# Weight conversion through PSUM banks, and decay and mask products in 64-row form, in an attention and two-expert-layer kernel

## The chip, the cores and the metric

The kernel runs on one core of a Trainium2 chip. A core has five engines with a queue each: TensorE (PE in the rows; its weight loads are PEld), VectorE (DVE), ScalarE (ACT), GpSimd (POOL) and SyncE (SP), which here issues the DMA transfers. SBUF is the working memory, PSUM holds TensorE's sums in eight banks. The metric is the device time of one execution in microseconds (us).

## The reference

```python
scores = scale * np.matmul(q, k.transpose(0, 1, 3, 2))      # 4 batches, 8 heads, 576 x 576, head size 64
cum = np.cumsum(np.log(np.clip(f, 0.0001, 1.0)), axis=-1)
scores = np.where(causal, -1e9, scores + cum[..., :, None] - cum[..., None, :])
attn = softmax(scores)                                      # over the last axis
x = (attn @ v)  ->  [2304, 512]                             # tokens by 8 heads x 64
h = np.maximum(x @ w_in, 0.0); x = h * h @ w_out            # w_in [512, 2048], w_out [2048, 512]
# router: logits + softplus(x @ w_noise) * noise, the two best of 8 experts per token
out[mask] += top2_w * (np.maximum(x[mask] @ w1[e], 0.0) @ w2[e])
```

## The kernel before

Every matrix is carried as a high and a low part in 16 bits (hi and lo), and a product is three matmuls: hi x hi, hi x lo, lo x hi (`HL3`). The program has three parts that overlap.

**Attention.** The first 256 queries of each batch are done by head units (`hd_tick`: `hd_s`, `hd_split`, `hd_pv`; 12 of them), the other 320 by units of two heads and 128 queries, or 64 for the last (`att_tick`: `att_s`, `att_exp`, `att_split`, `att_pv`; 48 of them). A unit's scores of its two heads (z = 0, 1) lie in two PSUM banks: three key products per head with 64 rows (contraction over the head size), then the decay product, whose 24 rows hold the three 16-bit pieces of the cumulated logarithms of 8 heads (`crow`) and a selector (`esel`), then the causal mask, an identity times a triangle (`identb`, `masku`, 128 rows). In units of 64 queries a bank holds both heads, side by side in partitions, for half of the keys. VectorE takes the maximum, ScalarE the exponential, GpSimd the low part, a DMA transposes, and TensorE multiplies by v.

**First layer.** `w_in` and `w_out` come as 64-bit floats in blocks, two halves for each of 16 values of i (`load_w`, SyncE). `conv_w` makes a 32-bit float of each from its two words in three VectorE steps (lines 434 to 436), with a scratch tile `w32` in SBUF, the result in place in the load's buffer `w64`; ScalarE makes the high part (line 443) and VectorE the low part (line 444). There are three load buffers. Ten of the 32 conversions are issued with the first head units (`weights_ahead`), the rest ahead of the steps that use them. `mm1` and `mm2` then go over chunks of 384 tokens and i: passes over chunk 0 and 1 with i from 0 to 7 (pass 0 and 1), again with i from 8 to 15 (pass 2 and 3), then one pass for each of the chunks 2 to 5.

**Router and experts.** From the end of the first layer on, after about 650 us; the change does not touch them.

The scores' banks are the pool tag "S" with three buffers, which rotate; at the start two more (tag "X") join, and `start_bank` and `main_bank` hand them out. A scheduler at build time sets the order of the instructions on each engine from the program's order, its dependences and its pools; each engine then runs its queue in that order.

Of the kernel before, what the change touches and what calls it, by code (L numbers as in the profile page):

```python
# [52 lines left out]
def attn_moe_moe_kernel(ctx: ExitStack, tc, qka, qk, v, f, w_io, wgn, noise, w1, w2, out):  # L53
# [59 lines left out]
    nc.gpsimd.affine_select(identb, identb, [[-1, 128]], ALU.not_equal, 1.0, base=0, channel_multiplier=1)  # L113
    nc.gpsimd.memset(masku, 0.0)
    nc.gpsimd.affine_select(masku, masku, [[-1, 128]], ALU.is_ge, -BIG, base=0, channel_multiplier=1)

# [22 lines left out]
    for z in range(2):  # L139
        es = esel[64 * z:64 * z + 24]  # L140
        nc.gpsimd.memset(es, -8.0)
        nc.gpsimd.affine_select(es, es, [[-3, 8], [0, 128]], ALU.is_ge, 0.0, base=0, channel_multiplier=1)
        nc.gpsimd.affine_select(es, es, [[3, 8], [0, 128]], ALU.is_ge, 0.0, base=2, channel_multiplier=-1)
    ident2k = consts.tile([128, 128], F16, name="ident2k")
# [32 lines left out]
    def att_s(u, pools):  # L177
        b, i, p = u
        n = p
        st[u] = [pool.tile([128, 512], F32, name="ps", tag=tag, bufs=bufs) for pool, tag, bufs in pools]  # L180
        q0 = S + 128 * i - HEAD
        if i < 4:
            N = 128 * (i + 1)
            for x, (qi, ki) in enumerate(HL3):
                for z in range(2):
                    r = slice(64 * z, 64 * z + 64)
                    nc.tensor.matmul(st[u][z][:, :N], QK[n][r, qi, q0:q0 + 128], QK[n][r, ki, :N], start=(x == 0), stop=False)  # L187
            for z in range(2):
                r = slice(64 * z, 64 * z + 24)
                nc.tensor.matmul(st[u][z][:, :N], esel[r, 2 * p + z], crow[r, b, :N], start=False, stop=False)  # L190
            for z in range(2):
                nc.tensor.matmul(st[u][z][:, N - 128:N], identb, masku, start=False, stop=True)  # L192
        else:
            for hf in range(2):
                ps = st[u][hf]
                ks = slice(288 * hf, 288 * hf + 288)
                for x, (qi, ki) in enumerate(HL3):
                    for z in range(2):
                        r = slice(64 * z, 64 * z + 64)
                        nc.tensor.matmul(ps[r, :288], QK[n][r, qi, q0:q0 + 64], QK[n][r, ki, ks], start=(x == 0), stop=False, skip_group_check=True)  # L200
                nc.tensor.matmul(ps[:, :288], esel.rearrange("r h t -> r (h t)")[0:24, 256 * p + 64:256 * p + 192], crow[0:24, b, ks], start=False, stop=(hf == 0), skip_group_check=True)
            for z in range(2):
                r = slice(64 * z, 64 * z + 64)
                nc.tensor.matmul(st[u][1][r, 224:288], identb[r, 64 * z:64 * z + 64], masku[r, 64 * z:64 * z + 64],
                                 start=False, stop=True, skip_group_check=True)

# [130 lines left out]
    def hd_s(u, bank):  # L337
# [13 lines left out]
        for p in range(np_):  # L351
            for z in range(2):
                r = slice(64 * z, 64 * z + 24)
                nc.tensor.matmul(ps[z][:, W * p:W * p + W], esel[r, 2 * (np_ * a + p) + z], crow[r, b, 0:W],
                                 start=False, stop=False, skip_group_check=True)
        v4 = [t.rearrange("p (c w) -> p c w", w=W) for t in ps]
        for z in range(2):
            nc.tensor.matmul(v4[z][:, :, 128 * i:128 * i + 128], identb, masku[:, None, :].to_broadcast([128, np_, 128]),
                             start=False, stop=True, skip_group_check=True)
        if a == 0:  # L360
# [451 lines left out]
    def weights_ahead(j):  # L812
        if j >= 0 and j % 2 == 0 and j // 2 < AHEAD:
            load_w(j // 2)
        if j >= 1 and (j - 1) // 2 < AHEAD:
            conv_w(("in", "out")[(j - 1) % 2], (j - 1) // 2)

# [36 lines left out]
    for s_i, (n, c, i) in enumerate(steps):  # L854
# [29 lines left out]
        for w_i in new:  # L884
            with ExitStack() as behind:
                if w_i >= NA and k:
                    behind.enter_context(tc.issue_after(seen[units[k - 1]]))
                conv_w("in", w_i)
                conv_w("out", w_i)
        if c in (2, 3) and i % 4 == 3:  # L890
# [138 lines left out]
```

## Time and profile before

| what | value |
|---|---|
| median of 3 runs | 1088.98 us (1086.57 to 1092.2) |
| the profiled execution | 1083.63 us, span 1081.9 us |
| TensorE busy | 991.0 us, 92% of the span |
| VectorE busy | 579.6 us, 54% |
| ScalarE, GpSimd busy | 443.3 us and 369.3 us |
| moved by DMA | 153.5 MB, mean 142 GB/s |

Busy time is what the engine's instructions cover of the span, not work at full speed: a matmul's end is modelled, and it includes the way through the array. The mean over the span hides that the first 200 us and the rest have different limits.

### The profile page before, as it was taken

The page shows a single profiled execution, that of the slowest core. Times are in us where ns is not written, and L with a number is a line of the kernel's source. Part 1 is how long each engine was busy: PE and PEld are TensorE (multiplying, and loading weights), DVE is VectorE, ACT ScalarE, POOL GpSimd, SP SyncE. Part 2 cuts the span into 40 slices and gives each one's busy share as a digit, 9 for nine tenths or more (in the row PEclk, how much of TensorE's full clock was granted, in tenths as well). Part 3 has the DMA queues.
Part 4 walks back from the last instruction along what each step waited for, and adds up shares of the span by engine and source line. Part 5 has one row for each costly group of instructions (what it writes and reads, how often), then busy time and mean ns, then how long its engine had stood idle before and what let it go on. Part 6 is the DMA issues. An engine that isn't in the chain of part 4 may idle for free.

```text
span 1081.9 us, 18041 instructions
## 1 busy us (share of the span) xinstructions
PE 991.0 (92%) x7050; PEld 537.5 (50%) x7050; DVE 579.6 (54%) x1159; ACT 443.3 (41%) x989; POOL 369.3 (34%) x331
## 2 busy tenths in 40 slices
PE   3748898899999999999998989998999999999996
PEld 1425444455454554555454434446646474646563
DVE  8998899624766666665537614214734343433121
ACT  3756676644555554564336312003513131412020
POOL 7454632311546535623410230533232404030202
PEclk9999899999999999999999989999999999999999
DMA  7599999433766784672529462437995938370303
GB/s 275 162 201 194 264 224 232 104 76 77 146 141 145 186 176 86 135 144 36 93 40 311 156 155 59 69 69 153 322 214 160 210 93 214 97 148 10 49 1 50
DMA packets 240393, 153.50 MB, mean 142 GB/s; under 512 B 194066, under 2 KB 204626, under 8 KB 240306
## 3 DMA queue, kind: packets, MB, share of 16 engines
q1 hardware_dynamic: 230194, 131.32, 50.3%
q0 software_dynamic: 10112, 21.02, 10.4%
q8 instruction: 56, 0.92, 0.4%
q14 instruction: 31, 0.25, 0.1%
HBM read 81.63 MB, written 24.30 MB: 98 GB/s over the span
## 4 chain that ended last, share of the span: by engine, by line
PE 62%; DVE 16%; DMA 9%; issue 6%; ACT 3%; POOL 2%; SPq 1%; ACTq 0%; POOLq 0%; DVEq 0%
PE e L753 18%; PE e L740 16%; PE m L456 10%; PE acc L500 9%; DMA wr<-in_w_dram 3%; DMA w<-in_w_io_dram 2%; DVE w L435 2%; PE ps L187 2%; DVE w L436 1%; DVE w L434 1%; PE po L282 1%; DVE r L466 1%; DVE wout L444 1%; DVE sm L217 1%; PE ps L200 1%
## 5 line engine op out<-in xcount | busy, mean ns | idle before, releaser
L740 PE MATMUL e<-xgT,w1s 128*128 128x320 f16 (+2 forms) x1536 | 217.8, 302 | 7.1 <-DMA xgT<-xg 5.0
L456 PE MATMUL m<-xT,win 128*128 128x384 f16 x1152 | 209.7, 332 | 13.7 <-ACT r L460 13.1
L500 PE MATMUL acc<-wout,g 128*128 128x512 f16 x864 | 205.6, 380 | 11.2 <-DVE g L464 6.3
L753 PE MATMUL e<-w2s,hT 128*128 128x512 f16 x960 | 212.1, 380 | 3.9 <-ACT hT L744 3.9
L740 PEld LDWEIGHTS <-w1s 128*128 128x128 f16 x1536 | 143.5, 99 | 80.7 <-issue 13.7
L456 PEld LDWEIGHTS <-win 128*128 128x128 f16 x1152 | 110.0, 99 | 88.8 <-issue 23.3
L753 PEld LDWEIGHTS <-hT 128*128 128x128 f16 x960 | 93.7, 98 | 114.0 <-ACT hT L744 4.2
L500 PEld LDWEIGHTS <-g 128*128 128x128 f16 x864 | 81.8, 98 | 102.2 <-DVE g L464 10.8
L744 ACT ACTIVATE hT<-e 128x320 f16<-128x320 f32 (+2 forms) x128 | 53.9, 435 | 186.3 <-PE e L740 186.2
L757 POOL DMA_INDIRECT out_dram<-y,tix x40 | 63.9, 1598 | 142.9 <-DVE y L756 134.7
L745 DVE SCALAR_TENSOR_TENSOR hT<-e,hT 128x320 f16<-128x320 f32 (+2 forms) x128 | 60.4, 487 | 96.0 <-ACT hT L744 95.8
L756 DVE TENSOR_SCALAR y<-e,gs 128x512 f32<-128x512 f32 x40 | 30.0, 750 | 146.0 <-PE e L753 131.6
L466 DVE TENSOR_TENSOR r<-r 128x384 f32<-128x384 f32 x64 | 56.8, 888 | 90.7 <-ACT g L461 90.7
L241 POOL TENSOR_TENSOR phl<-pr,phl 128x384 f16<-128x384 f32 (+1 forms) x64 | 68.7, 1090 | 81.6 <-issue 59.8
L460 ACT ACTIVATE r<-m 128x384 f32<-128x384 f32 x96 | 46.6, 486 | 90.9 <-PE m L456 85.4
L706 POOL DMA_INDIRECT xg<-x2d,tix x40 | 44.7, 1117 | 113.4 <-DMA xgT<-xg 103.5
L641 POOL DMA_INDIRECT table<-ent,si x36 | 36.1, 1002 | 127.8 <-DVE si L638 99.0
L676 ACT ACTIVATE w2s<-wr 128x1024 f16<-128x1024 f32 x32 | 32.5, 1050 | 106.3 <-PE e L753 88.5
L217 DVE TENSOR_REDUCE sm<-ps 128x1 f32<-128x384 f32 (+2 forms) x96 | 51.7, 561 | 34.0 <-PE ps L192 20.8
L220 ACT ACTIVATE pr<-ps,sm 128x384 f32<-128x384 f32 (+1 forms) x64 | 40.0, 627 | 57.7 <-DVE sm L219 56.1
L349 PE MATMUL psab<-hs 64*128 64x128 f16 (+1 forms) x192 | 27.7, 342 | 26.2 <-ACT pr L371 14.7
L461 ACT ACTIVATE g<-r 128x384 f16<-128x384 f32 x96 | 50.2, 522 | 1.8
(253 smaller groups left out, 1160.0 us busy)
## 6 DMA issues: line engine op xcount, KB each, us to landing
wr<-in_w_dram SPq DMA_DIRECT2D x64, 512.0 KB
w<-in_w_io_dram SPq DMA_DIRECT2D x32, 512.0 KB
qkr<-in_qk_dram SPq DMA_DIRECT2D x16, 448.0 KB
vr<-in_v_dram SPq DMA_DIRECT2D x16, 320.0 KB
x2d<-x SPq DMA_DIRECT2D x18, 256.0 KB
qkh<-in_qka_dram SPq DMA_DIRECT2D x8, 512.0 KB
out_dram<-zero SPq DMA_DIRECT2D x5, 768.0 KB
vh<-in_v_dram SPq DMA_DIRECT2D x8, 256.0 KB
```

The source lines that it names most:

```text
L217: seen[u] = nc.vector.tensor_reduce(sm[:, z:z + 1], ps[z][:, :N], AX.X, ALU.max).ins
L241: nc.gpsimd.tensor_tensor(lo, pv, hi, op=ALU.subtract)
L456: nc.tensor.matmul(ps, win[i][:, cc, wi, :], xT[:, xi, cc, r0:r0 + CH], start=(x == 0), stop=(x == 11))
L460: nc.scalar.activation(r, ps, AF.Relu)
L461: nc.scalar.activation(g[:, 0, :], r, AF.Square, scale=2.0 ** -10)
L466: nc.vector.tensor_tensor(r, r, r, op=ALU.mult)
L500: nc.tensor.matmul(acc[t], g[:, gi, 128 * t:128 * t + 128], wout[i][:, wi, :], start=(i in ends[c][0] and x == 0), stop=(i in ends[c][1] a ...
L740: nc.tensor.matmul(ps[:, :hw], w1s[:, cc, wi, 128 * i:128 * i + 128], xgT[:, 4 * xi + cc, hw * q:hw * q + hw], start=(x == 0), stop=(x == 11))
L744: nc.scalar.activation(hi, ps[:, :hw], AF.Relu)
L745: nc.vector.scalar_tensor_tensor(hT[:, i, 1, hw * q:hw * q + hw], ps[:, :hw], 0.0, hi, op0=ALU.max, op1=ALU.subtract)
L753: nc.tensor.matmul(ps, hT[:, i, hi, 128 * j:128 * j + 128], w2s[:, i, wi, :], start=(i == 0 and x == 0), stop=(i == NFE - 1 and x == 2))
L757: s_ = nc.gpsimd.indirect_dma_start(out=out, out_offset=bass.IndirectOffsetOnAxis(ap=tix[:, j, 0:1], axis=0), in_=y, in_offset=None, compu ...
```

## The change

It does three things. The conversion's scratch and its result go to a PSUM bank, taken from `start_bank` or `main_bank` as the scores take theirs; so `w32` is gone, the load's buffer is only read, and ScalarE and VectorE read the result from PSUM. The decay product gets 64 rows instead of 24: `crow` is cleared first, so that the rows 24 to 63 of each half add nothing, and the selector is one column per head, repeated over the 128 (or 64) columns of the weight load by its access pattern. The mask product is split in two halves of 64 rows, the identity and the triangle lying in each half of the partitions. The low parts of the probabilities are made on GpSimd, as before.

```diff
-    identb = consts.tile([128, 128], BF16, name="identb")
-    masku = consts.tile([128, 128], BF16, name="masku")
-    esel = apool.tile([128, H, 128], F16, name="esel")
+    identb = consts.tile([128, 2, 128], BF16, name="identb")
+    masku = consts.tile([128, 2, 128], BF16, name="masku")
+    esel = apool.tile([128, H], F16, name="esel")
     crow = apool.tile([128, B, S], F16, name="crow")
+    nc.gpsimd.memset(crow, 0.0)
...
+    def decay(r, h, m):
+        return esel[r, h:h + 1].to_broadcast([64, m])
...
             for z in range(2):
-                r = slice(64 * z, 64 * z + 24)
-                nc.tensor.matmul(st[u][z][:, :N], esel[r, 2 * p + z], crow[r, b, :N], start=False, stop=False)
-            for z in range(2):
-                nc.tensor.matmul(st[u][z][:, N - 128:N], identb, masku, start=False, stop=True)
+                r = slice(64 * z, 64 * z + 64)
+                nc.tensor.matmul(st[u][z][:, :N], decay(r, 2 * p + z, 128), crow[r, b, :N], start=False, stop=False)
+            for hf in range(2):
+                for z in range(2):
+                    r = slice(64 * z, 64 * z + 64)
+                    nc.tensor.matmul(st[u][z][:, N - 128:N], identb[r, hf], masku[r, hf], start=False, stop=(hf == 1))
...
-                nc.tensor.matmul(ps[:, :288], esel.rearrange("r h t -> r (h t)")[0:24, 256 * p + 64:256 * p + 192], crow[0:24, b, ks], start=False, stop=(hf == 0), skip_group_check=True)
+                for z in range(2):
+                    r = slice(64 * z, 64 * z + 64)
+                    nc.tensor.matmul(ps[r, :288], decay(r, 2 * p + z, 64), crow[r, b, ks], start=False, stop=(hf == 0), skip_group_check=True)
...
-    def conv_w(kind, i):
+    def conv_w(kind, i, bank):
         t = wst.pop((kind, i))
-        u = astream.tile([128, 512], I32, name="w32", bufs=1)
+        w_ = bank()
+        u = w_.bitcast(I32)
         nc.vector.tensor_scalar(u, t[:, :, 1], 3, 0x3FFFFFF8, op0=ALU.logical_shift_left, op1=ALU.bitwise_and)
         nc.vector.scalar_tensor_tensor(u, t[:, :, 1], -0x40000000, u, op0=ALU.bitwise_and, op1=ALU.bitwise_or)
-        nc.vector.scalar_tensor_tensor(t[:, :, 0], t[:, :, 0], 29, u, op0=ALU.logical_shift_right, op1=ALU.bitwise_or)
-        w_ = t.bitcast(F32)[:, :, 0]
+        nc.vector.scalar_tensor_tensor(u, t[:, :, 0], 29, u, op0=ALU.logical_shift_right, op1=ALU.bitwise_or)
```

The head units (`hd_s`) get the same two changes as the units of 128 queries. Lines after the constants stand some 7 to 12 lines further down in the changed kernel (434 to 436 and 444 are 447 to 449 and 456 there).

On VectorE, where pass 1 begins (the conversions of i = 8 and 9; w64 is the load's buffer, w32 the scratch, sm and ps belong to an attention unit), the order before is:

```order
L435 SCALAR_TENSOR_TENSOR w32_1602<-w64_1538,w32_1602 128x512
L217 TENSOR_REDUCE sm_1713<-ps_1702 128x1
L219 TENSOR_SCALAR sm_1713<-sm_1713 128x1
L436 SCALAR_TENSOR_TENSOR w64_1538<-w64_1538,w32_1602 128x512
L219 TENSOR_SCALAR sm_1713<-sm_1713 128x1
L434 TENSOR_SCALAR w32_1608<-w64_1540 128x512
L435 SCALAR_TENSOR_TENSOR w32_1608<-w64_1540,w32_1608 128x512
L444 SCALAR_TENSOR_TENSOR win8_155<-w64_1538,win8_155 128x4x128
L436 SCALAR_TENSOR_TENSOR w64_1540<-w64_1540,w32_1608 128x512
```

and in the changed kernel (psab are banks of the scores, here taken by conversions, xs and vs belong to the attention):

```order
L447 TENSOR_SCALAR psab_1635<-w64_1569 128x512
L447 TENSOR_SCALAR psab_1641<-w64_1571 128x512
L229 TENSOR_SCALAR sm_1627<-sm_1627 128x1
L448 SCALAR_TENSOR_TENSOR psab_1635<-w64_1569,psab_1635 128x512
L448 SCALAR_TENSOR_TENSOR psab_1641<-w64_1571,psab_1641 128x512
L449 SCALAR_TENSOR_TENSOR psab_1635<-w64_1569,psab_1635 128x512
L447 TENSOR_SCALAR psab_1682<-w64_1647 128x512
L449 SCALAR_TENSOR_TENSOR psab_1641<-w64_1571,psab_1641 128x512
L309 TENSOR_TENSOR xs_1514<-po_1435,sums_1197 128x512
L178 SCALAR_TENSOR_TENSOR vs_1729<-vr_1600,vs_1729 128x10x64
L448 SCALAR_TENSOR_TENSOR psab_1682<-w64_1647,psab_1682 128x512
```

A conversion's first step now stands before the last step of up to two others, each with a bank of its own, and no attention unit's maximum stands between them.

On TensorE, in a unit of 64 queries late in the attention (set is q and k of a head pair, ps the two banks of the unit), the order before is:

```order
L200 MATMUL ps_4123<-set2_1693 64x288
L201 LDWEIGHTS esel_98
L201 MATMUL ps_4123<-crow_99,esel_98 128x288
L200 LDWEIGHTS set2_1693
L200 MATMUL ps_4124<-set2_1693 64x288
```

and in the changed kernel:

```order
L209 MATMUL ps_4198<-set2_1726 64x288
L212 LDWEIGHTS esel_98
L212 MATMUL ps_4198<-crow_99,esel_98 64x288
L212 LDWEIGHTS esel_98
L212 MATMUL ps_4198<-crow_99,esel_98 64x288
L209 LDWEIGHTS set2_1726
L209 MATMUL ps_4199<-set2_1726 64x288
```

The decay product of 128 partitions between key products of 64 has become two of 64 partitions, in the same shape as the products around it.

On TensorE, in a unit of 128 queries in the second pass over chunk 0 before, and in pass 1 in the changed kernel (ps_2110 and ps_2111 are the banks of one unit's two heads, ps_1857 is the bank of one head), the order before is:

```order
L187 MATMUL ps_2110<-set0_1561 128x512
L187 LDWEIGHTS set0_1561
L187 MATMUL ps_2111<-set0_1561 128x512
L190 LDWEIGHTS esel_98
L190 MATMUL ps_2110<-crow_99,esel_98 128x512
L190 LDWEIGHTS esel_98
L190 MATMUL ps_2111<-crow_99,esel_98 128x512
L192 LDWEIGHTS identb_96
L192 MATMUL ps_2110<-masku_97,identb_96 128x128
L192 LDWEIGHTS identb_96
L192 MATMUL ps_2111<-masku_97,identb_96 128x128
```

and in the changed kernel:

```order
L194 MATMUL ps_1857<-set2_1726 128x384
L194 LDWEIGHTS set2_1726
L194 MATMUL ps_1857<-set2_1726 128x384
L194 LDWEIGHTS set2_1726
L194 MATMUL ps_1857<-set2_1726 128x384
L197 LDWEIGHTS esel_98
L197 MATMUL ps_1857<-crow_99,esel_98 128x384
L201 LDWEIGHTS identb_96
L201 MATMUL ps_1857<-masku_97,identb_96 128x128
L201 LDWEIGHTS identb_96
L201 MATMUL ps_1857<-masku_97,identb_96 128x128
```

Before, the two heads' products alternate; in the changed kernel one head's key, decay and mask products stand alone here, with two mask products for one.

## Rows read from the trace of the kernel before

**Rows 1.** stretches: length, busy us (instructions) of PE, PEld, DVE, ACT, POOL, clock, DMA
```profile
25.00:61.00 36.00, 21.67 (x144) 12.48 (x145) 33.29 (x46) 20.14 (x62) 18.97 (x8) 1.00 0.58 163
61.00:122.00 61.00, 44.93 (x352) 25.35 (x352) 54.06 (x75) 41.01 (x114) 29.65 (x19) 0.95 1.05 224
122.00:200.00 78.00, 70.83 (x529) 35.77 (x528) 71.76 (x128) 51.34 (x118) 26.18 (x22) 0.98 0.85 212
200.00:513.00 313.00, 304.70 (x2584) 159.59 (x2583) 178.72 (x466) 166.91 (x398) 129.57 (x130) 1.00 0.57 123
```

**Rows 2.** SyncE's waits from 14 to 216 us: total, times, longest
```profile
SPq L428 <- DVE wout L444: 17.1, 9, 5.0
SPq L428 <- DVE win L444: 14.3, 6, 9.7
```

**Rows 3.** VectorE's timeline, 37 to 52 us: start, duration, instruction
```profile
42.09 2.49 DVE L435 SCALAR_TENSOR_TENSOR w<-w,w 128x512 int32<-128x512 int32 x1
44.50 0.68 DVE L366 TENSOR_REDUCE smh<-psab 128x2 f32<-128x512 f32 x1
...
50.01 0.69 DVE L435 SCALAR_TENSOR_TENSOR w<-w,w 128x512 int32<-128x512 int32 x1
```

**Rows 4.** GpSimd's timeline, 36 to 52 us
```profile
39.12 4.91 POOL L327 TENSOR_TENSOR hs<-qkh,hs 128x1024 f16<-128x1024 f32 x2
43.99 5.10 POOL L381 TENSOR_TENSOR phlh<-pr,phlh 128x1024 f16<-128x1024 f32 x2
```

**Rows 5.** single lines: count, ns least/median/most, first and last start
```profile
L434 DVE TENSOR_SCALAR w<-w x32: 408/426/2336, 14.3 to 193.8; 128x512 int32<-128x512 int32 x32
...
L435 DVE SCALAR_TENSOR_TENSOR w<-w,w x32: 642/692/2494, 14.9 to 194.7; 128x512 int32<-128x512 int32 x32
...
L444 DVE SCALAR_TENSOR_TENSOR wout<-w,wout x16: 678/685/2617, 24.8 to 198.2; 128x512 f16<-128x512 f32 x16
...
L366 DVE TENSOR_REDUCE smh<-psab x24: 673/678/692, 26.0 to 123.1; 128x2 f32<-128x512 f32 x16, 128x4 f32<-128x512 f32 x8
...
L479 DVE SCALAR_TENSOR_TENSOR sp<-acc,sp x6: 678/683/692, 156.9 to 203.3; 128x512 f16<-128x512 f32 x6
...
L456 PE MATMUL m<-xT,win x1152: 322/326/528, 88.9 to 643.4; 128*128 128x384 f16 x192
```

**Rows 6.** VectorE's conversion steps (tile w) by stretch
```profile
14.00:61.00 47.00, 33.02 (x29) 1.00 0.60 178
61.00:122.00 61.00, 33.19 (x35) 0.95 1.05 224
122.00:200.00 78.00, 46.82 (x64) 0.98 0.85 212
sum 186.00, DVE 113.03; mean DVE 37.68
```

**Rows 7.** TensorE's timeline, a unit of 128 queries
```profile
301.31 0.82 PE L187 MATMUL ps<-set 64*128 64x512 f16 x6
302.07 0.39 PE L190 MATMUL ps<-crow,esel 24*128 24x512 f16 x2
302.39 0.28 PE L192 MATMUL ps<-masku,identb 128*128 128x128 bf16 x2
```

**Rows 8.** TensorE's timeline, a head unit, one head alone
```profile
95.05 0.83 PE L349 MATMUL psab<-hs 64*128 64x256 f16 x6
95.81 0.39 PE L354 MATMUL psab<-crow,esel 24*128 24x256 f16 x2
```

**Rows 9.** TensorE's timeline, a unit of 64 queries
```profile
343.79 0.29 PE L201 MATMUL ps<-crow,esel 24*128 24x288 f16 x1
344.01 0.55 PE L200 MATMUL ps<-set 64*64 64x288 f16 x6
```

**Rows 10.** the chain that ended last, 212 to 217 us: start, us, what
```profile
214.11 1.94 PE acc L500 x9
```

**Rows 11.** TensorE's waits, 27 to 216 us: total, times, longest
```profile
PE psab L349 <- ACT pr L371: 14.7, 4, 7.5
```

More of the change, by code (lines that the diff above doesn't have):

```diff
@@ L139, in attn_moe_moe_kernel @@
     for z in range(2):
[L140 removed]
+        es = esel[64 * z:64 * z + 64]
         nc.gpsimd.memset(es, -8.0)
[L142 to L143 removed]
+        nc.gpsimd.affine_select(es, es, [[-3, 8]], ALU.is_ge, 0.0, base=0, channel_multiplier=1)
+        nc.gpsimd.affine_select(es, es, [[3, 8]], ALU.is_ge, 0.0, base=2, channel_multiplier=-1)
+    def decay(r, h, m):
+        return esel[r, h:h + 1].to_broadcast([64, m])
     ident2k = consts.tile([128, 128], F16, name="ident2k")
@@ L200, in att_s @@
                         nc.tensor.matmul(ps[r, :288], QK[n][r, qi, q0:q0 + 64], QK[n][r, ki, ks], start=(x == 0), stop=False, skip_group_check=True)
-                nc.tensor.matmul(ps[:, :288], esel.rearrange("r h t -> r (h t)")[0:24, 256 * p + 64:256 * p + 192], crow[0:24, b, ks], start=False, stop=(hf == 0), skip_group_check=True)
+                for z in range(2):
+                    r = slice(64 * z, 64 * z + 64)
+                    nc.tensor.matmul(ps[r, :288], decay(r, 2 * p + z, 64), crow[r, b, ks], start=False, stop=(hf == 0), skip_group_check=True)
             for z in range(2):
                 r = slice(64 * z, 64 * z + 64)
-                nc.tensor.matmul(st[u][1][r, 224:288], identb[r, 64 * z:64 * z + 64], masku[r, 64 * z:64 * z + 64],
-                                 start=False, stop=True, skip_group_check=True)
+                nc.tensor.matmul(st[u][1][r, 224:288], identb[r, 0, 0:64], masku[r, 0, 0:64], start=False, stop=True, skip_group_check=True)
     def att_exp(u):
@@ L352, in hd_s @@
             for z in range(2):
-                r = slice(64 * z, 64 * z + 24)
-                nc.tensor.matmul(ps[z][:, W * p:W * p + W], esel[r, 2 * (np_ * a + p) + z], crow[r, b, 0:W],
+                r = slice(64 * z, 64 * z + 64)
+                nc.tensor.matmul(ps[z][:, W * p:W * p + W], decay(r, 2 * (np_ * a + p) + z, 128), crow[r, b, 0:W],
                                  start=False, stop=False, skip_group_check=True)
         v4 = [t.rearrange("p (c w) -> p c w", w=W) for t in ps]
-        for z in range(2):
-            nc.tensor.matmul(v4[z][:, :, 128 * i:128 * i + 128], identb, masku[:, None, :].to_broadcast([128, np_, 128]),
-                             start=False, stop=True, skip_group_check=True)
+        for hf in range(2):
+            for z in range(2):
+                r = slice(64 * z, 64 * z + 64)
+                nc.tensor.matmul(v4[z][:, :, 128 * i:128 * i + 128], identb[r, hf], masku[r, hf, None, :].to_broadcast([64, np_, 128]),
+                                 start=False, stop=(hf == 1), skip_group_check=True)
         if a == 0:
@@ L815, in weights_ahead @@
         if j >= 1 and (j - 1) // 2 < AHEAD:
-            conv_w(("in", "out")[(j - 1) % 2], (j - 1) // 2)
+            conv_w(("in", "out")[(j - 1) % 2], (j - 1) // 2, start_bank)
     turn = [0]
@@ L887, in attn_moe_moe_kernel @@
                     behind.enter_context(tc.issue_after(seen[units[k - 1]]))
-                conv_w("in", w_i)
-                conv_w("out", w_i)
+                conv_w("in", w_i, main_bank)
+                conv_w("out", w_i, main_bank)
         if c in (2, 3) and i % 4 == 3:
```

5 lines of the change are left out of this document (3 added, 2 removed).

## Prediction

> **What bounds the kernel now.** I read the table of stretches first, since no share of the whole span says where a change inside the first fifth is felt [rows 1]. Up to 61 us VectorE is the busy one: 33.3 of 36 us, with TensorE at 21.7 and the DMA engines at 0.58. From 61 to 122 us VectorE has 54.1 of 61 us, but the DMA share is 1.05, so the transfers are full as well. From 122 to 200 us three things stand close together: VectorE 71.8 of 78, TensorE 70.8, DMA 0.85. From 200 to 513 us TensorE has 304.7 of 313 us and nobody else is over 0.6. So this program has a VectorE stage, a DMA stage, a mixed stage and a TensorE stage, and each part of the change must be priced in the stage where it falls. After 513 us the change touches nothing but a few attention units.
>
> The waits of SyncE's queue come next: its weight loads (L428) stood 17.1 and 14.3 us on the last conversion step, L444, for a free buffer [rows 2]. The queue is in order, so transposes for the attention stand behind these loads. Then VectorE's timeline, beside GpSimd's: a conversion step takes 0.69 us (L435 at 50.01) or 2.49 us (L435 at 42.09), and the long ones end when GpSimd's tensor operation ends (hs, 39.12 to 44.03), while a reduction that reads PSUM keeps 0.68 us in the midst of GpSimd work (44.50) [rows 3, 4]. The spread is the same for the other steps: minimum 0.41 to 0.68, maximum 2.0 to 2.6 us, while the 24 reductions of 512 columns out of PSUM keep 673 to 692 ns and the six operations with one PSUM and one SBUF input 678 to 692 ns [rows 5].
>
> **Part 1, conversion through PSUM.** Each of the 32 conversions keeps its four VectorE steps. The three with two SBUF inputs (L435, L436, L444) get one SBUF and one PSUM input; the first (L434) writes PSUM. No row of before shows VectorE writing PSUM. Bounds: the nearest rows are the ones with a PSUM input, 0.68 to 0.69 us [rows 5]; the lower end is L434's own 0.41; the upper end is today's mean, the 113 us that 128 steps take, 0.88 us each [rows 6]. I take 0.69 for all four, since the element count is the same 512.
>
> A rule speaks against the change: the Trainium skill, "VectorE: DVE Perf Modes", Why PSUM operands drop a tier, has any PSUM operand cost an fp32 operation its double speed. The rows bear it out as far as they go (L434 has 0.41 us in SBUF, what touches PSUM 0.68 or more). By that loss alone, with no stall relieved, 32 steps x 0.28 us would be 9 us more and the time 1090; the 0.69 above holds the loss already.
>
> By stage, busy time of these steps now against steps x 0.69 [rows 6]: to 61 us 33.0 against 29 x 0.69 = 20.0, 13.0 off; 61 to 122 us 33.2 against 35 x 0.69 = 24.2, 9.0 off; 122 to 200 us 46.8 against 64 x 0.69 = 44.2, 2.6 off. Together 24.6 us of VectorE. How much is on the path: to 61 us VectorE is the bound at 92% and the load buffers come free one step earlier, so 11 us (13 less the idle twelfth, rounded down). From 61 to 122 us the DMA engines are full whatever VectorE does; I give 2 of 9. From 122 to 200 us I give 3: 2.6, and a little for the earlier buffer. A load buffer is let go after the third step instead of the fourth, and L444 stands behind a ScalarE copy, so the 31 us of queue waits [rows 2] shrink; what is late next is the DMA itself. Sum 16 us. ScalarE's copy (L443) now reads PSUM; it is off the path and I price it at nothing: VectorE's next conversion hides it.
>
> **What part 1 adds.** A bank of the scores (three in the main part, five at the start) is held from the first step to the last. VectorE's order shows it: in pass 1 three conversions stand open at once (psab_1635, 1641, 1682), which is all three banks. Behind a conversion that waits for a bank stand the products g, for which TensorE's L500 waits. And scores that get one bank at a time are issued one head after the other. That costs TensorE: two heads alternating put six 512-column products into 0.76 us (301.31 to 302.07), one head alone puts six of 256 columns into the same 0.76 us (95.05 to 95.81) [rows 7, 8]. Along TensorE's order, 83 of the 192 key products of the later units are followed by one of the other head before, 44 after.
>
> **Part 2, the 64-row form.** When consecutive products use another tiling of the array, the next one starts late: the decay product of 288 columns starts at 343.79, the next at 344.01, 0.22 us later, and 288 columns are 0.12 us at the pitch of nine 512-column products in 1.94 us (0.42 ns a column); 0.10 us is the switch. Likewise decay to mask: 302.07 to 302.39 is 0.32 us, of which two heads at once need 0.21 [rows 7, 9, 10]. In the order in which TensorE's products stand I count 388 changes of tiling before and 214 after; 174 x 0.10 = 17.4 us less. Against that stand the masks, now two 64-row products per head instead of one of 128 rows: the 12 early groups stream 8 x 512 and 16 x 256 columns a second time, the 32 later units 64 x 128, together 16,384 columns or 7 us if no heads alternate, about 5 as they stand in the order; and the lost alternation, 39 places, about 4 us. Walking the whole order with 0.42 ns a column, 0.10 us a switch and alternating heads side by side gives 938.8 us of TensorE before and 931.1 after: 7.7 us less. Of it 6.4 us lie in the passes of chunks 2 to 4, within the TensorE stage, where they count in full; the rest is work that moves from pass 1 into passes 2 and 3. I take 8 us. (The small items, crow's memset of 2304 columns, two more selects, and esel's long fill and selects gone from GpSimd, lie within the first 20 us beside VectorE and count as nothing; uncovered they are a gain of a few us.) The 120 more weight loads run beside products.
>
> **Sum.** 11 + 2 + 3 + 8 = 24 us. The profiled execution took 1083.6 us (span 1081.9), the median of the three runs is 1089.0, 5 us above it. 1083.6 - 24 = 1059.6; on the scale of the runs 1065.
>
> **Rivals.** (a) The relief is not on the path: DMA sets the pace from 61 us on and what the first stage gains is waited for there; then only TensorE's 8 us and some 4 us of the 16 remain: 1077. For it speaks the DMA share of 1.05; against it the 0.58 before 61 us, into which work can move forward. (b) The relief runs through: all 24.6 us of VectorE and the queue waits behind it, and TensorE's switches without the lost pairs (+4): about 24.6 + 8 + 4 + 5 of queue waits = 42 us, 1047. (c) PSUM steps are not cheap: a step that reads and writes the same bank takes today's mean of 0.88 us. Then part 1 gives 0 and part 2 gives 8: 1081. (d) Slower: banks. TensorE already stood 14.7 us on four waits for a bank that ScalarE's exponentials had not let go, 3.7 us each [rows 11]. Every conversion now needs such a bank and holds it. If two in five of the 32 conversions wait as long, 13 x 3.7 = 48 us stand on VectorE, and by the shares above (16 of 24.6, 65%) 31 of them on the path: 1089 - 24 + 31 = 1096. It decides at 10 of 32 conversions (10 x 3.7 x 0.65 = 24 us); below that some gain stands. For it speaks that all three banks are open at once; against it that VectorE has other work ordered between.
>
> **How the numbers follow.** Chances: forecast 0.46, (a) 0.18, (b) 0.16, (c) 0.08, (d) 0.12. A difference under 0.5% (5.4 us) is about what a measurement of this kernel can't tell from none: 1083.5 to 1094.4 is "the same". The forecast and (b) are faster; (a) is faster in nearly all of its width; (c) splits, half faster, half the same; (d) is half the same, half slower. Faster 0.80, same 0.13, slower 0.07. The range: low end at (b), 1045; high end just under (d), 1088; it leaves out some 2 in 10.
>
> **What would show it.** Right: L434's successor at 0.6 to 0.7 us and no conversion step over 0.8; VectorE less busy before 61 us; loads issued without waiting for the last step; no row with 32- or 24-row products, the 0.10 us gaps within a unit gone; the first product of L456 (88.9 us now [rows 5]) some 10 us earlier. Wrong: conversion steps that start late behind ScalarE's exponentials, TensorE waiting for VectorE's conversion at the key products, or a DMA share still over 1 with the first product of L456 where it was.

## The result and the profile after

The changed kernel takes 1051.7 us (median of 4 runs, 1050.4 to 1055.32) against 1088.7 us for the kernel before on the same chip: a ratio of 0.966, 95% interval 0.963 to 0.970, 37 us faster. The forecast was 1065 in a range of 1045 to 1088, so the direction and the range held, and the gain was half as large again as the 24 us of the sum. The profiled execution of the changed kernel has a span of 1050.0 us, 31.9 us under that of before; the other 5 us are that the profiled execution of before stood 5 us under its median, as the prediction noted.

The stretches of the changed kernel, in the columns of [rows 1]:

```profile
25.00:61.00 36.00, 18.75 (x154) 13.48 (x154) 25.51 (x48) 21.50 (x67) 15.30 (x8) 0.53 0.98 241
61.00:122.00 61.00, 52.10 (x417) 31.70 (x414) 42.63 (x71) 41.20 (x111) 28.23 (x19) 0.77 0.99 209
122.00:200.00 78.00, 74.96 (x529) 39.74 (x529) 62.38 (x114) 50.60 (x112) 17.99 (x15) 1.00 0.68 175
200.00:513.00 313.00, 305.43 (x2836) 170.86 (x2835) 189.28 (x497) 176.07 (x426) 147.58 (x153) 1.00 0.63 133
```

VectorE is down from 33.3 to 25.5 us, from 54.1 to 42.6 and from 71.8 to 62.4, and the DMA share before 61 us is up from 0.58 to 0.98: transfers moved forward, as forecast. The four VectorE steps of the conversion, by line (count, ns least/median/most, first and last start):

```profile
L447 DVE TENSOR_SCALAR psab<-w x32: 675/689/696, 13.6 to 191.7; 128x512 int32<-128x512 int32 x32
...
L448 DVE SCALAR_TENSOR_TENSOR psab<-w,psab x32: 683/691/700, 14.3 to 192.9; 128x512 int32<-128x512 int32 x32
...
L449 DVE SCALAR_TENSOR_TENSOR psab<-w,psab x32: 678/687/698, 15.1 to 194.0; 128x512 int32<-128x512 int32 x32
...
L456 DVE SCALAR_TENSOR_TENSOR win<-psab,win x16: 637/683/692, 16.4 to 192.3; 128x512 f16<-128x512 f32 x16
L456 DVE SCALAR_TENSOR_TENSOR wout<-psab,wout x16: 680/688/694, 20.7 to 195.4; 128x512 f16<-128x512 f32 x16
```

All 128 steps take 0.64 to 0.70 us; none is stretched to the 2.3 to 2.6 us that [rows 5] had. SyncE's loads now wait for the third step (total, times, longest, 14 to 216 us):

```profile
SPq L440 <- DVE psab L449: 27.7, 11, 5.3
...
SPq L440 <- DMA w<-in_w_io_dram: 6.9, 2, 4.9
```

27.7 us against 31.4 in [rows 2]: the wait moved to an earlier step and hardly shrank. With every other wait of these loads in the same stretch it is 38.8 us against 43.2. TensorE's waits behind the first main product, first of before (88 to 216 us), then of the changed kernel (77 to 216 us):

```profile
PE m L456 <- ACT r L460: 5.9, 5, 1.9
PE acc L500 <- DVE g L464: 5.1, 4, 3.1
PE acc L500 <- DVE sm L219: 1.7, 1, 1.7
```

```profile
PE po L410 <- DMA pth<-phlh: 3.6, 1, 3.6
PE po L292 <- DVE psab L449: 1.6, 1, 1.6
PE m L468 <- ACT r L472: 1.1, 1, 1.1
```

What is to be seen: TensorE's 5.1 us for VectorE's g and 4.8 of the 5.9 us for ScalarE's r are gone. One wait for a conversion is new, 1.6 us. Before the first main product there is a longer one. The head units' key products take their banks from the conversions too (changed kernel, 27 to 216 us):

```profile
PE psab L359 <- DVE win L456: 6.3, 2, 6.1
PE psab L359 <- ACT pr L383: 6.1, 2, 3.2
```

TensorE waiting there for a conversion is one of the signs of being wrong that the prediction names, and it came true. It didn't turn the result, since the wait for ScalarE's exponentials at the same products fell from 14.7 us [rows 11] to 6.1.

To place the gain I took, in each kernel's trace, the start of the first of each 96 first-layer products (`mm1`): the passes of the front part follow one another there. The table has the profiled executions in us, and the ratio of the timed runs to the kernel before.

| kernel | pass 0 | pass 1 | chunk 2 | chunk 5 | span | ratio (95%) |
|---|---|---|---|---|---|---|
| before | 88.9 | 145.2 | 279.2 | 568.4 | 1081.9 | |
| changed | 77.4 | 133.8 | 262.0 | 538.5 | 1050.0 | 0.966 (0.963 to 0.970) |
| conv_only | 80.8 | 137.8 | 271.3 | 558.8 | 1075.0 | 0.983 (0.979 to 0.987) |
| rows_only | 82.0 | 139.1 | 270.9 | 548.1 | 1060.0 | 0.978 (0.975 to 0.981) |
| loads4 | 97.0 | 151.8 | 286.0 | 573.8 | 1093.6 | 1.003 (1.001 to 1.005) |
| mask128 | 72.6 | 127.7 | 254.0 | 545.7 | 1060.2 | 0.974 (0.971 to 0.977) |
| heads_apart | 80.3 | 136.4 | 265.7 | 549.7 | 1061.6 | 0.978 (0.975 to 0.981) |
| mix | 73.1 | 128.6 | 256.9 | 533.4 | 1048.9 | 0.963 (0.960 to 0.966) |
| esel_small | 86.7 | 143.6 | 279.4 | 567.5 | 1082.1 | 0.995 (0.993 to 0.997) |
| banks2 | 76.3 | 131.4 | 257.6 | 535.4 | 1046.6 | 0.963 (0.960 to 0.966) |
| changed_again | 79.5 | 135.4 | 263.6 | 543.6 | 1054.9 | 0.966 (0.963 to 0.969) |
| start_sb | 81.9 | 133.9 | 262.1 | 540.6 | 1053.2 | 0.967 (0.964 to 0.969) |
| rows_mix | 89.2 | 146.8 | 278.5 | 560.9 | 1071.4 | 0.984 (0.980 to 0.987) |
| paired | 73.4 | 128.4 | 251.9 | 530.7 | 1042.9 | 0.959 (0.956 to 0.961) |

Of the 31.9 us, 17.2 come before chunk 2, 12.7 in chunks 2 to 4, 2.0 after. changed_again is the same program as changed, on another chip: two executions differ by 2 us in the passes and 5 in the span, so a single column is worth no more than that, and a verdict below goes by the ratio. The profiled execution of conv_only was the slowest of its four, 3 us over their median, while that of before was 5 us under: by their spans its gain is 7 us, by the runs 18.

Between pass 0 and chunk 2, before takes 190.3 us, conv_only 190.5, rows_only 188.9, the changed kernel 184.6 and changed_again 184.1. So there either half of the change alone gains next to nothing, and the two together some 6 us. Pass 0 itself begins 8.1 us earlier in conv_only, 6.9 in rows_only, 11.5 in the changed kernel and 9.4 in changed_again.

### The profile page after: what moved, and what is told of

It is laid out like the page before. It is cut to its first block, busy times and chain, and to the rows that moved or that the text cites. A ratio compares the mean times of both kernels' runs of the same rounds, so it can differ in the third digit from the quotient of the medians.

```text
span 1050.0 us, 18267 instructions
## 1 busy us (share of the span) xinstructions
PE 970.7 (92%) x7170; PEld 545.8 (52%) x7170; DVE 543.6 (52%) x1159; ACT 443.7 (42%) x989; POOL 353.9 (34%) x334
## 4 chain that ended last, share of the span: by engine, by line
PE 68%; DMA 10%; DVE 8%; issue 5%; ACT 5%; POOL 2%; SPq 2%; ACTq 0%; DVEq 0%; POOLq 0%
PE e L765 18%; PE e L752 17%; PE m L468 12%; PE acc L512 11%; DMA wr<-in_w_dram 3%; PE ps L194 2%; DMA w<-in_w_io_dram 2%; PE po L292 2%; DMA pth<-phlh 1%; PE ps L209 1%; DVE r L478 1%; SPq L720 1%; POOL table L653 1%; ACT pr L230 1%; PE ps L197 1%
## 5 line engine op out<-in xcount | busy, mean ns | idle before, releaser
L468 PE MATMUL m<-xT,win 128*128 128x384 f16 x1152 | 205.5, 329 | 8.4 <-ACT r L472 7.7
L752 PEld LDWEIGHTS <-w1s 128*128 128x128 f16 x1536 | 143.2, 98 | 79.5 <-issue 11.0
L251 POOL TENSOR_TENSOR phl<-pr,phl 128x384 f16<-128x384 f32 (+1 forms) x64 | 65.6, 1039 | 106.8 <-issue 85.2
L478 DVE TENSOR_TENSOR r<-r 128x384 f32<-128x384 f32 x64 | 46.3, 724 | 97.0 <-ACT g L473 86.5
```

The source lines that it names most:

```text
L251: nc.gpsimd.tensor_tensor(lo, pv, hi, op=ALU.subtract)
L468: nc.tensor.matmul(ps, win[i][:, cc, wi, :], xT[:, xi, cc, r0:r0 + CH], start=(x == 0), stop=(x == 11))
L478: nc.vector.tensor_tensor(r, r, r, op=ALU.mult)
L752: nc.tensor.matmul(ps[:, :hw], w1s[:, cc, wi, 128 * i:128 * i + 128], xgT[:, 4 * xi + cc, hw * q:hw * q + hw], start=(x == 0), stop=(x == 11))
```

## The experiments

**conv_only**: before, with `conv_w` through the banks, decay and masks left alone.

```diff
-        u = astream.tile([128, 512], I32, name="w32", bufs=1)
+        w_ = bank()
+        u = w_.bitcast(I32)
...
```

> The kernel before with the conversion through PSUM banks alone; decay and mask products as before. Additive theory (each part pays in its stage): the start gain of 11.5 us and the 9.1 us of pass 1 appear here in full, chunks 2 to 4 gain nothing: 1088.7 - 21 = 1068, within 4. First rival (the two parts need each other: the single-headed order that the banks force costs TensorE switches, which the 64-row form then makes cheap): the start still gains 11, but the chunks 2 to 4 lose some 4 us where heads no longer alternate, 1072 or more. Second rival (the gain of pass 1 comes from the cheaper tilings, not from the conversion): pass 1 gains under 3 us and the time is about 1076. By every theory all 128 conversion steps take 0.68 to 0.70 us.

Measured: 0.983, 18 us faster (14 to 22); 7.9 us of it in the profile before chunk 2, 1.6 in chunks 2 to 4. All steps take 0.64 to 0.71 us. VectorE's busy time from 60 to 200 us is 107.6 us against 126.8, and TensorE's wait for g from 77 to 216 us is 1.0 us. The additive theory had 21 us: within the interval, but the 9.1 us of pass 1 did not stay. Pass 1 is 7.0 us shorter and the two passes behind it are 6.5 longer, so that from pass 0 to chunk 2 it takes as long as before, though VectorE is that much freer; what it keeps lies before pass 0. TensorE waits for transposes instead, where before had 3.6 us (77 to 216 us):

```profile
PE po L398 <- DMA pth<-phlh: 11.8, 3, 6.0
```

**rows_only**: the changed kernel with its conversion back in SBUF.

```diff
-        w_ = bank()
-        u = w_.bitcast(I32)
+        u = astream.tile([128, 512], I32, name="w32", bufs=1)
...
```

> The changed kernel with the conversion back in SBUF; only decay and mask products are in the 64-row form. Additive theory: chunks 2 to 4 start and end 12 us closer together than before, the first product of L468 of pass 0 stays at 88.9 within 1 us, 1088.7 - 13 to 16 = 1073 to 1076. First rival (the parts need each other): the masks in two halves stream more columns and with two heads alternating the switches are fewer to begin with, so no more than 6 us in chunks 2 to 4: 1082. Second rival (pass 1's 9 us are TensorE's switches): 1066, with 9 us in pass 1. Conversion steps stay at a mean of 0.88 us by all.

Measured: 0.978, 24 us faster (21 to 27). None of the three had it whole. The second rival had the time (1066; 1065 measured), and pass 1 is 6.9 us shorter, but the two passes behind it give 4.6 back, so that most of this work was moved and not saved. The additive theory had the 11.9 us in chunks 2 to 4. The 8.3 us before chunk 2, nearly all of them before pass 0, nobody had. With conv_only the two parts make 42 us apart and 37 together, so they overlap by some 5 us, about the width of the intervals.

**loads4**: before, with four load buffers.

```diff
-            t = astream.tile([128, 512, 2], I32, name="w64", tag="w64", bufs=3)
+            t = astream.tile([128, 512, 2], I32, name="w64", tag="w64", bufs=4)
...
```

> The kernel before with four load buffers in place of three; its conversion stays in SBUF, with its stalls. If the start's gain comes from buffers that come free earlier (the loads' 31 us of waits, and the transposes queued behind them), the first product of L456 of pass 0 comes 5 to 11 us earlier and the time is 1078 to 1084. If it comes from VectorE's time (13 us less before 61 us), the start moves by under 2 us, VectorE is still over 90% busy there, and the time is 1087 to 1090.

Measured: 1.003, slower by 3 us (1 to 5), and the first main product 8 us later. TensorE's waits, 77 to 216 us:

```profile
PE psab L349 <- ACT pr L371: 13.2, 3, 6.7
PE acc L500 <- DVE g L464: 10.0, 4, 4.6
```

The wait for VectorE's g is 10.0 us where before had 5.1. The loads' waits are 40.3 us where before had 43.2 (14 to 216 us). So one buffer more gives nothing, but it doesn't take the waits away either: the run doesn't show what buffers that come free earlier would give.

**mask128**: the changed kernel, each head's mask again one product of 128 rows.

```diff
-            for hf in range(2):
-                for z in range(2):
-                    r = slice(64 * z, 64 * z + 64)
-                    nc.tensor.matmul(st[u][z][:, N - 128:N], identb[r, hf], masku[r, hf], start=False, stop=(hf == 1))
+            for z in range(2):
+                nc.tensor.matmul(st[u][z][:, N - 128:N], identw, maskw, start=False, stop=True)
...
```

> The changed kernel with each head's mask as one 128-row product of 128 columns a block, as before, and the decay in the 64-row form. By the prediction's terms: 16,384 fewer streamed columns are worth up to 5 to 7 us of TensorE, and the changes of tiling come back only where a 64-row product follows a mask: with some 60 places at 0.10 us, 6 us. So 1051.7 within 3, split as early groups faster and the later units slower. If the second halves of the masks run wholly beside another head's products, only the switches are felt: 1055 to 1060. If a switch costs nothing where a weight load is due anyway, only the columns are felt: 1046.

Measured: 0.974, 8 us slower than the changed kernel, with the split that was expected and larger sizes: 8 us ahead at chunk 2, 15 us lost in chunks 2 to 4. The same place of TensorE's queue shows one part of it, a unit of 384 columns whose heads are issued one after the other: before, in mask128, and in the changed kernel (start, duration, instruction).

```profile
389.03 0.66 PE L187 MATMUL ps<-set 64*128 64x384 f16 x3
389.62 0.33 PE L190 MATMUL ps<-crow,esel 24*128 24x384 f16 x1
389.88 0.23 PE L192 MATMUL ps<-masku,identb 128*128 128x128 bf16 x1
390.04 0.66 PE L187 MATMUL ps<-set 64*128 64x384 f16 x3
390.63 0.33 PE L190 MATMUL ps<-crow,esel 24*128 24x384 f16 x1
390.90 0.23 PE L192 MATMUL ps<-masku,identb 128*128 128x128 bf16 x1
390.96 0.31 PE L282 MATMUL po<-vs,pt 128*128 128x64 f16 x5
```

```profile
369.00 0.66 PE L201 MATMUL ps<-set 64*128 64x384 f16 x3
...
369.75 0.23 PE L206 MATMUL ps<-maskw,identw 128*128 128x128 bf16 x1
369.91 0.66 PE L201 MATMUL ps<-set 64*128 64x384 f16 x3
...
370.73 0.34 PE L297 MATMUL po<-vs,pt 128*128 128x64 f16 x6
```

```profile
368.75 0.68 PE L194 MATMUL ps<-set 64*128 64x384 f16 x4
369.25 0.32 PE L197 MATMUL ps<-crow,esel 64*128 64x384 f16 x1
369.27 0.32 PE L194 MATMUL ps<-set 64*128 64x384 f16 x1
369.41 0.22 PE L201 MATMUL ps<-masku,identb 64*128 64x128 bf16 x1
369.43 0.32 PE L194 MATMUL ps<-set 64*128 64x384 f16 x1
369.47 0.22 PE L201 MATMUL ps<-masku,identb 64*128 64x128 bf16 x1
369.59 0.32 PE L197 MATMUL ps<-crow,esel 64*128 64x384 f16 x1
369.76 0.27 PE L201 MATMUL ps<-masku,identb 64*128 64x128 bf16 x2
369.96 0.41 PE L292 MATMUL po<-vs,pt 128*128 128x64 f16 x8
```

The unit takes 1.93 us before (389.03 to 390.96), 1.73 in mask128, 1.21 in the changed kernel. In the queue, as the program is built, the order is the same: three key products, decay and mask of the first head, then those of the second. In the changed kernel the fourth of the first four key products is the second head's first, and its other two start among the first head's decay (369.25) and masks (369.41, 369.47): they run on the other half of the rows ahead of products that stand before them in the queue. So TensorE doesn't run its queue wholly in order, as the section on the kernel before says of every engine. With a mask of 128 rows between the heads, the second head starts behind it (369.75 and 369.91). The overlap is not the whole of the 15 us: the table in the next section gives it 3.8, less 3.4 for the columns that mask128 saves.

**heads_apart**: the changed kernel, with every 128-query unit issued head after head.

```diff
-            for x, (qi, ki) in enumerate(HL3):
-                for z in range(2):
...
+            for z in range(2):
+                r = slice(64 * z, 64 * z + 64)
+                for x, (qi, ki) in enumerate(HL3):
...
```

> The changed kernel with the two heads of every 128-query unit issued one wholly after the other (key products, decay, mask halves of the first, then of the second). In the changed kernel one unit that stood in this order already took 1.21 us from 368.753 to 369.960, the same unit in mask128 1.74 and before 1.94. New theory (a 64-row product starts as soon as its half of the array is free, ahead of products that stand earlier in the queue and wait for the other half, so heads overlap whatever their order, as long as nothing of 128 rows stands between): the units keep 1.2 us, and the time is 1051.7 within 4. The prediction's rule (products start in the order of the queue, so a head issued alone pays its columns alone): some 40 more key-product places of the later units lose their partner, 0.5 us and more a unit, 1058 to 1064, with the loss in chunks 2 to 4.

Measured: 0.978, 13 us slower than the changed kernel, with 7.5 us of it in chunks 2 to 4. The time is that of the prediction's rule, the trace that of the new theory:

```profile
374.86 0.68 PE L194 MATMUL ps<-set 64*128 64x384 f16 x4
375.36 0.32 PE L195 MATMUL ps<-crow,esel 64*128 64x384 f16 x1
375.37 0.32 PE L194 MATMUL ps<-set 64*128 64x384 f16 x1
...
376.07 0.32 PE L288 MATMUL po<-vs,pt 128*128 128x64 f16 x5
```

The heads overlap again and the unit takes 1.21 us (374.86 to 376.07). But the first two key products run alone, and a unit whose heads alternate takes 0.87 us (442.90 to 443.77 in the changed kernel): so the order still costs 0.34 us a unit. The second head's first product started when three products of the first head stood waiting before it (decay and two masks), here and in the changed kernel; in these rows none passes more. The theory is right in kind and wrong that the order doesn't matter. Of the 7.5 us, 3.3 are lost overlap and 0.8 switches, by the table in the next section; the rest are waits and the lower clock.

**mix**: the changed kernel, with the 128-row mask in the early groups (`hd_s`) alone.

```diff
...
-                nc.tensor.matmul(v4[z][:, :, 128 * i:128 * i + 128], identb[r, hf], masku[r, hf, None, :].to_broadcast([64, np_, 128]),
-                                 start=False, stop=(hf == 1), skip_group_check=True)
...
+            nc.tensor.matmul(v4[z][:, :, 128 * i:128 * i + 128], identw, maskw[:, None, :].to_broadcast([128, np_, 128]),
+                             start=False, stop=True, skip_group_check=True)
```

> The changed kernel with the 128-row mask in the early groups alone; the later units keep their mask in two 64-row halves. If mask128's two parts add (pass 2 began at 166.9 there against 173.6 in the changed kernel, and chunks 2 to 4 took 291.7 us there against 276.5): 1051.7 - 6.7 = 1045. If the lead of 4.8 us that mask128 had at the first product of pass 0 is a chance of how the start falls out, not a price of the halves in the early groups: 1050 to 1053. The later units' overlap is untouched in both: chunks 2 to 4 take 276 to 278 us.

Measured: 1046.75 us, 0.963; 5.1 us ahead of the changed kernel at chunk 2, and 276.5 us for chunks 2 to 4. The intervals of the two kernels overlap, so the profile alone carries the 5 us.

**esel_small**: before, with `esel` one column per head, on 24 rows.

```diff
-    esel = apool.tile([128, H, 128], F16, name="esel")
+    esel = apool.tile([128, H], F16, name="esel")
...
```

> The kernel before, with esel as 8 columns that the weight load repeats, so that its fill and two selects on GpSimd (1.94 + 3.18 + 2.76 us for 1024 columns) become short; its rows stay 24, and the 64-query units take their decay product head by head. Asked: why rows_only, whose conversion is that of before, had its first main product at 82.0 and not at 88.9. If it is the GpSimd work at the start, which the prediction priced at nothing: the first product of L456 comes at 82 to 85, and the time falls by 3 to 6 us, to 1083 to 1086. If it is TensorE's cheaper tilings at the start: it stays at 88 to 90, and the time within 2 us of before.

Measured: 0.995, 6 us faster (3 to 8), but the first main product comes at 86.7 and the profiled span is that of before. So the short fill, with the split decay products of the 64-query units that the run needs, is worth a few us in the timed runs; the profile doesn't show where, or which of the two, and neither explains rows_only's 82.0.

**banks2**: the changed kernel, each conversion holding two banks.

```diff
-        w_ = bank()
-        u = w_.bitcast(I32)
+        w_, s_ = bank(), bank()
+        u = s_.bitcast(I32)
...
```

> The changed kernel with two banks of the scores for each conversion in place of one (the third step writes the second). Rival (d) of the prediction, bank waits of 3.7 us each: if banks are what limits the rest, twice the demand costs 20 us or more (1072 to 1090), with TensorE waiting at the key products for conversions, in passes 0 and 1 above all. If the scheduler has room for them, under 6 us: 1052 to 1058.

Measured: 1047.2 us, 0.963. Twice the demand for banks costs nothing. Rival (d) is dead.

**changed_again**: no edit.

> The changed kernel once more, without an edit: how far one execution's start differs from another's, and its time beside the three below on one chip. heads_apart has the same instructions in the same order until pass 1 and had its first main product at 80.3 where the changed kernel had 77.4. Expected: 77 to 81 for that product, 1050 to 1053 for the time. A first product at 73 or 85 would make the start's differences between the variants worthless.

Measured: 1055.56 us where the kernel before took 1092.76, the same ratio of 0.966, and the first main product at 79.5.

**paired**: mix, with both heads' first key products ahead of the rest.

```diff
...
+                    if x == 0:
+                        for mm in both:
+                            behind.enter_context(tc.issue_after(mm.ins))
...
```

> mix, with the two heads of each 128-query unit held together: every key product but the first of each head is queued behind the first products of both, so that all 32 units alternate (23 of the changed kernel's stand head after head). An alternating unit of 384 columns takes 0.50 + 0.37 = 0.87 us in the changed kernel, one head after head 1.21. If only TensorE's time counts: 23 x 0.34 = 8 us less, 1047 - 8 = 1039. If the second bank's wait then stands on TensorE, or the units take the place of products that would have filled it, no gain or a loss: 1045 to 1055, with waits for ScalarE's exponentials at the key products.

Measured: 1047.08 us, 0.959 (0.956 to 0.961) of before; the changed kernel on the same chip took 1055.56, 0.966 (0.963 to 0.969). The best of all, and outside the changed kernel's interval. Yet chunks 2 to 4 take 278.8 us, no less than mix's 276.5: the 5 us that it is ahead of mix lie before chunk 2, where it has done 103 of the later units' key products and mix 108. Alternating the last units' heads gains nothing there in sum: against mix 4.9 us more run beside others, but switches take 2.6 us more, and waits and the lower clock 4.3 (the table in the next section).

**start_sb**: the changed kernel, the first 10 conversions in SBUF.

```diff
-            conv_w(("in", "out")[(j - 1) % 2], (j - 1) // 2, start_bank)
+            conv_w(("in", "out")[(j - 1) % 2], (j - 1) // 2, None)
...
```

> The changed kernel with the first 10 of the 32 conversions back in SBUF (those before the main part), the other 22 through PSUM. If the conversion pays at the start alone, as the prediction's largest term has it: the first main product comes at 82 (rows_only 82.0) and the time is about that of rows_only, 1062 to 1066. If it pays in passes 0 and 1 (9.1 us less in pass 1): 1052 to 1057.

Measured: 0.967, the time of the changed kernel. The first main product comes at 81.9, as in rows_only; at pass 1 the lag is gone (133.9 against 133.8 and 135.4). With the 64-row form the conversion pays through the 22 of the main part, by which start_sb differs from rows_only (0.967 against 0.978; 180.2 us against 188.9 from pass 0 to chunk 2), not through the ten at the start. With the 24-row form, in conv_only, the profile has it the other way round.

**rows_mix**: mix with the conversion back in SBUF.

```diff
-        w_ = bank()
-        u = w_.bitcast(I32)
+        u = astream.tile([128, 512], I32, name="w32", bufs=1)
...
```

> mix with the conversion back in SBUF: 64-row decay everywhere, masks of 128 rows in the early groups and in halves in the later units. Additive: 1046.8 + 13.4 (rows_only less the changed kernel) = 1060. If the early groups' 128-row masks gain their 5 us only where the start is no longer held by VectorE: 1064 to 1067, first main product at 81 to 84.

Measured: 0.984, 18 us faster than before, 6 us behind rows_only. The first product comes at 89.2: the 128-row early masks, which are 5 us ahead at chunk 2 with the conversion in the banks, are 8 behind there without it.

One view sets rows_mix, loads4 and before apart from the rest: the key products of the later units that stand in pass 0 (length, PE busy and count, PEld, clock, DMA). Before, then the changed kernel, then rows_mix (PE alone):

```profile
88.88:145.24 56.36, 3.95 (x21) 1.24 (x21) 0.94 1.04 224
```

```profile
77.39:133.79 56.40, 1.32 (x6) 0.41 (x6) 0.87 0.90 186
```

```profile
89.24:146.82 57.58, 3.87 (x21) 0.94 1.04 223
```

21 in before, esel_small and rows_mix, 24 in loads4; 6 in the changed kernel, conv_only, rows_only, mix and start_sb. The four that start more of the later units in pass 0 let TensorE wait 4.6 to 10.0 us for VectorE's g from 77 to 216 us (8.8 in rows_mix), the others 0 to 4.2. All of the listed kernels have done 105 to 108 of these products by chunk 2. This could mean that part of what the change gains before chunk 2 is a build-time order that puts attention off until VectorE is free. The table speaks against it: with 6 such products in pass 0, conv_only and rows_only take 190.5 and 188.9 us from pass 0 to chunk 2, about as long as before's 190.3 and loads4's 189.0. The order wasn't tried by itself.

## Why the prediction was right, and where its terms were not

**Conversion steps at 0.69 us: right.** The median is 0.69, the longest 0.70. The rule of the Trainium skill that the prediction weighed ("VectorE: DVE Perf Modes", Why PSUM operands drop a tier) shows in the first step, 0.41 us in [rows 5] and 0.69 now; the stalls that went outweigh it. One reading was loose: the long step at 42.09 ends at 44.58, 0.55 us after GpSimd's operation and not with it [rows 3, 4].

**Part 1, 16 us: the sum held, in part by luck.** conv_only measures 18 us (14 to 22). Of its stages the first was read as VectorE's alone, 11 us, and conv_only's first main product does come 8.1 us earlier. But rows_only's comes 6.9 us earlier with the conversions of before, and start_sb takes the banks away from just those ten conversions at no cost in time. The failed step is "to 61 us VectorE is the bound": it was not the only one. That TensorE's own products stand in the chain is likely and not shown. They ran at the lower clock, in the changed kernel too (0.53 from 25 to 61 us), as a head unit's timeline of before shows:

```profile
31.75 1.43 PE L349 MATMUL psab<-hs 64*128 64x256 f16 x6 [7.54 <-ACT pr L371]
33.12 0.60 PE L354 MATMUL psab<-crow,esel 24*128 24x256 f16 x2
```

From the second on, the six start 213 ns apart, 0.83 ns a column, twice the 0.42 of [rows 10]. That is the 1.2 GHz level, though [rows 1] gives 1.00 for this stretch. The first main product also marks less work in the changed kernel: 44 of the early groups' decay products stand before it, 52 in before. The 2 and 3 us for 61 to 200 us were too small for the changed kernel: start_sb and rows_only show that the conversions pay there, and VectorE's busy time from 60 to 200 us is 11.3 us less than in rows_only (117.3 to 106.0) at about as many instructions (183 and 186). conv_only, whose passes gain nothing, shows that VectorE's time alone is not enough for it.

**Part 2, 8 us: mis-sized, 24 alone.** In chunks 2 to 4 the forecast had 6.4 and rows_only shows 11.9. Chunk 3 is the cleanest place, at full clock in both kernels; before, and changed:

```profile
374.98:469.17 94.19, 92.00 (x813) 48.16 (x807) 58.71 (x142) 50.27 (x121) 44.87 (x45) 1.00 0.63 131
```

```profile
354.92:444.48 89.56, 88.71 (x836) 49.50 (x831) 55.79 (x143) 50.13 (x121) 44.08 (x45) 1.00 0.65 137
```

4.6 us less. I took from each product's start to the next the columns at 0.42 ns. What is left over by 60 to 150 ns is a switch, more is a wait or the lower clock, and less, or below nothing, is overlap: products that run beside others. In chunk 3 the switches fall from 76 with 7.7 us to 46 with 4.5, so 0.10 us a switch was right. All of chunks 2 to 4, in us:

| kernel | columns | switches | overlap | waits, lower clock | sum |
|---|---|---|---|---|---|
| before | 268.3 | 22.4 | -14.7 | 13.1 | 289.1 |
| changed | 275.0 | 13.5 | -20.1 | 8.1 | 276.5 |
| changed_again | 275.0 | 13.4 | -20.0 | 11.6 | 280.0 |
| rows_only | 274.2 | 13.3 | -19.6 | 9.4 | 277.3 |
| mask128 | 271.6 | 14.6 | -16.3 | 21.8 | 291.7 |
| heads_apart | 275.0 | 14.3 | -16.8 | 11.6 | 284.1 |
| mix | 275.0 | 13.3 | -20.1 | 8.3 | 276.5 |
| paired | 275.3 | 15.9 | -25.0 | 12.6 | 278.8 |

From before to the changed kernel the switches give 8.9 us, the overlap 5.4 and the waits 5.0, and 6.7 us of columns come on top; changed_again says that the waits can be 3.5 us more in the same program. The wrong step is "the lost alternation, about 4 us": the walk let products start only in the order of the queue, so that fewer alternating places meant less overlap, while in 64-row form the heads overlap even when issued apart (1.93 to 1.21 us a unit), and the overlap grew. The Trainium skill, "TensorEngine Tiling (Array Packing)", Key Properties, has different tiles load weights and multiply in parallel; the trace agrees (369.25 and 369.27). mask128's chunks 3 and 4:

```profile
355.06:448.05 92.99, 90.63 (x820) 49.00 (x815) 60.36 (x142) 50.02 (x121) 44.92 (x45) 0.98 0.62 133
448.05:545.70 97.65, 93.75 (x847) 50.70 (x843) 52.66 (x137) 44.70 (x112) 31.52 (x36) 0.98 0.43 76
```

In all three chunks it is 15.2 us slower than the changed kernel. 3.8 of them are overlap that the 128-row mask cuts and 1.1 are switches, against 3.4 us of columns saved; the other 13.7 are waits and the lower clock, which mask128 has for 17 us there and the changed kernel not at all. What brings those about is not shown, and waits and clock alone can move one program by 3.6 us in one chunk: changed_again takes 93.2 us in chunk 3. The 8 us of the timed runs stand; that they are the overlap's is not shown. In the early groups the halves may cost: mix without them is 5 us ahead at chunk 2, by the profile alone.

**Rivals.** (a) fell: relief before chunk 2 was on the path. (b), 1047, is nearest to the result of 1051.7, but not by its mechanism: the queue's waits stayed at 27.7 us. (c) fell with 0.69 us. (d) fell with banks2. The forecast came out inside its range because the range reached down to (b): its own sum, 24 us, is two thirds of the 37.

**The small items, "nothing; uncovered a few us"**: esel_small measures 6 us (3 to 8), so they were not all covered, if that gain is GpSimd's.

**Open**: why rows_only's start is 7 us earlier than before's with the same conversions (esel's fill explains 2); why the conversions of the main part pay with the 64-row form and not without it; where mask128's waits come from; why the early 128-row masks help with the banks and hurt without; and how much the order of the later units is worth by itself. Each of these runs changes the build-time order, which no run held fixed.

## What to carry to other kernels

Keep a chain of small matmuls in one tiling, masks and corrections included: it saves the switches (8.9 us of the 12.7 in chunks 2 to 4), and it lets products of the two row halves overlap without being interleaved by hand, which about pays for the columns that are streamed twice; a 128-row product between the heads kept them apart. Where VectorE and GpSimd both work in SBUF, moving one operand of the step to PSUM can pay (18 us in conv_only) although the step's best case gets slower. Price a start-up by removing the suspected cost there alone: the first main product moved 11.5 us where 11 were forecast, and that was no proof, since start_sb's moved 7.0 without the relief it was put down to, and the time was the same.

## What the runs showed of the hardware

That products of one half of the rows start ahead of queued ones of the other (three were passed at 369.1 us in the changed kernel) was not expected; nor that the clock column can say 1.00 where a known product's pitch (0.83 against 0.42 ns a column) shows the lower level; nor that a second bank for each conversion, from a pool of three in the main part, costs nothing (0.963 against 0.966).
